# Three of four block sums of the spatial weights by adding DMA transfers in place of VectorE sums, in a fused attention and gated-MLP block on one Trainium2 core

## The chip, the core and the metric

The kernel runs on one NeuronCore of a Trainium2 chip. Such a core has five instruction streams that run at the same time and meet only through semaphores: TensorE (PE, matrix products into the accumulator memory PSUM; PEld is its weight load), VectorE (DVE, elementwise work), ScalarE (ACT, activation functions and copies), GpSimd (POOL, slower elementwise work, and issuer of transfers) and SyncE (SP, which here only issues DMA transfers). The working memory, SBUF, has 128 partitions. All five queues are in order: an instruction that waits holds up everything behind it on its engine.

The metric is the device time of one execution in microseconds, from an execution without the profiler, as the median of several; lower is better. Before the change: 227.09 us, median of 3 runs (226.91 to 227.54). The profiled execution has a time of its own, given below.

## The reference

One sequence of 2048 tokens with 512 features goes through two residual blocks, all in bfloat16:

```python
def _A_ref(x, wqkv, wo):                     # linear attention, 32 heads of 16
    q, k, v = split(x @ wqkv)
    phi = lambda t: jnp.where(t > 0, t + 1, jnp.exp(t)) + 1e-06
    pq, pk = (phi(q), phi(k))
    kv = jnp.einsum('bhsd,bhse->bhde', pk, v)
    z = jnp.einsum('bhsd->bhd', pk)
    o = einsum(pq, kv) / (einsum(pq, z) + 1e-06)
    return merge_heads(o) @ wo

def _B_ref(x, w_in, w_sp, b_sp, w_out):      # gated MLP, F = 1792, Fh = 896
    z = _gelu(jnp.einsum('bsd,df->bsf', x, w_in))
    z1 = z[..., :Fh].copy()
    z2 = _layernorm(z[..., Fh:], axis=-1)
    g = jnp.einsum('ts,bsf->btf', w_sp, z2) + b_sp[None, :, None]
    return jnp.einsum('bsf,fd->bsd', z1 * g, w_out)

h  = x + _A_ref(_layernorm(x), A_wqkv, A_wo)
h2 = h + _B_ref(_layernorm(h), B_w_in, B_w_sp, B_b_sp, B_w_out)
```

The change lies in the product of w_sp (2048 x 2048, the spatial weights, which mix tokens) with z2 (2048 x 896).

## The kernel before

Tokens are cut into 16 tiles of 128. In the first 65 us or so the attention block is done, tile by tile. Then come the input product with the two halves of w_in (z2 with its normalisation, and z1), the spatial mixing with the gate, and the output product with w_out. The last three stages overlap.

**Fewer products by sums.** The large products use a form of Strassen's scheme (Winograd's variant): a 2 x 2 block product is made of 7 block products instead of 8, at the price of sums of blocks. For w_sp, a row of tokens n (0 to 7) is taken together with row n + 8. Their transposed weights lie in SBUF as the tiles wt[n] and wt[n + 8], each 128 x 2048: the first half of the columns (index 0 to 7 of a 128-block) and the second (8 to 15). The program calls the four blocks y11 (wt[n], first half), y21 (wt[n], second), y12 (wt[n + 8], first) and y22 (wt[n + 8], second). It forms four sums of 128 x 1024 elements each with the helper `comb` (L859, whose DVE instruction the profile shows at L863):

- S1 = y12 + y22, into a tile of its own, sa[c][0];
- S2 = S1 - y11, into a second tile of its own, sa[c][1] (called q2);
- S3 = y11 - y12, in place into y12;
- S4 = y21 - S2, in place into y11.

The other operand has its own sums: zt1, zt2, zt4 and an in-place one in z2 (`t_sums`, L962).

**Pairs of rows.** `mix(ia, ib, nest)` (L1055) does two rows at a time, c = 0 and 1, in the order 0, 1 | 2, 3 | 7, 4 | 5, 6 (`MIX`); "tile n" below is the row pair n, n + 8. Each row has three PSUM banks, B, A and E. Bank A first gets y11 times z2, a copy of it goes to B (ACT), E gets S1 times zt1, B gets S2 times zt2 added ("the q2 product"), and so on; the last product of row n is y11 (by then S4) times the high half of z2, into E. The gate, z1 * (g + b_sp), reads the banks on DVE (L999, L1007, L1008), and each gated tile z1[n] is then transposed by a DMA transfer issued from SP (zgT[n], which lies over wt[n]) for the output product.

**A second level.** With a bit set in `NEST` (0, 3, 15, 7 for the four calls), one of the seven products is done for both rows together by `nested` (L1030), which applies the same scheme once more, with 224-column products and sums of its own: bit 1 reads y11 of both rows, bit 2 reads S1 of both, bit 4 reads y21, bit 8 reads y22. With bit 2 its last sum is written over the first half of sa[1][0], that is, over S1 of the second row.

**Order of the work.** Every operation is recorded by a helper with what it reads and writes, a cost and, for a transfer, a latency. The order in which the operations stand on each engine's queue is not computed in the kernel: it is unpacked from the string `ORDER` (L16), a list of operation numbers; the waits follow from the recorded reads and writes. A transfer has a semaphore by its name, and two transfers of one name share it: the two halves of wt[n] do, so a reader of either half waits for both. Since helpers record, one line stands for many operations in the profile (L427 all products, L446 all activations, L863 all of `comb`).

**Queues around the change.** SP issues all loads, the transposing loads of wt (L460), the zgT transfers and the stores. POOL does the small statistics steps of the normalisations (L541 to L575) and has nothing to do once the normalisation of z2 is over. DVE does the block sums, the additions of PSUM (L866, L1039), the statistics, and the gate.

Of the kernel before, what the change touches and what calls it, by code (L numbers as in the profile page):

```python
# [15 lines left out]
ORDER = "c-jrt)1oB^5Cgz;I%n?Kwr$(CZQHhO+qP}nwrzWMf1#c#93lV+4?{%6MGnM6E;xk92p~2hfk=cX$cd=Pjl@WRI7o;*$crRMfr3biXo!zsNQq=9gj6Vue29+ZNR9jmLOE1Gc~nFtq(ft*L1h#`2oynDWI%c}L=1#RMl?YqWI`1bMP@WbGgL(uR7W-xLp5YYH*`TvG)E1zL@l&JSJXrc6i0WIKyCCuYmCDfltd}CL3WfuY1Bba)J0qLLM)6&S+v7g^hP~Qz(gFzB=kW)ghYEx#z9QM5!A;a9K|toKwmV#Gz7;0^v6I<MMsRl2`s^I48k&WLKrN^QcTBb48{s{#t^K;NX*1)tiu_M!f~uZD1^lt%)n?Yz$~oCd@RITJjGB9!)(mKGc3YJEXD?G!gFlL4s6C2oWxw5!cNS?3+%-%?7=?l#(tc|OB}!}oWoX}#|3P|6<owhyNYYLj+?lJOSp_1SZi<b8n^Kt5AXr2>>cjlF7D$E?jg8^uyytk5p2C}uulkS5$z$?*jKE!ZwO<5@EO1H2$Ae3!dhs1j4ybCQ1%zF@A!de_6z?I-olv~EvCh?s20QAvRG`BMX{`w+5#5Yf>|2NX4x&sa#&tlZqY5R6|i`g&(c{=OJun$v8}N5R>tC5e9K@3t*phdBv#%ES$<1s8LhAtu?kkv5?DPeXGN`&)wWDl+3HwQYh}f(xYf7Z*4C0+Pit){tbtXry4KE0Su*QmsjRA{v^JL6df76oW(_Tm9kTY;!46vq`)Z|ag!Q$Nw$B<_NgHjAt+!3LBi7G4+9>O9W9+Cku^Cp=YS}EiYu{|P-M0PK)W%v1J7~vkoE@{7Hs0pg2^(N7ZGu&|JNCft*+V;N2kg6bvQswE?%N}KY^SY;4YX!9$S&F;cDBKG$>!QC`)%{=wf(gDcG<ev4{L5i?24VS1@^{BaFPwPvv!78?U%*kAA9>hduGO9Y<9H(Gtt@IV)C8E<zM?}L+y#3vtV3kSttfEINw_w#^VPYZapkMC)+jaW>YO3&s%sVU=Ai{2!6DumX#?Ofm7_6EwX8rjS;!TK3OehXD(i_NKDB*%*l|<$LF@#u3Kc@uux3J)XdEn)|Gi#gI$=PODzp+vLFlarWImc)@EqdVK=5_Le}F;>&3#{Xo(nwpRF{Dus(ZplXYhgmSJKx=VnXCvb<#txW#(1FT-#Eqp}6du@AQ~J-^siYsr2r%I%!PBuvUyoW*Sxjm6lX85ox3If&7@gB3WNtyz(SS&2Kjivu~A4OyJ?xtqy2gl#yK^SIp>a2Ut3EqB;LzGG!BVhJ{4V`k(^e&BE(V@aOi2#(`UTg>+y$yF@H@odK>tiq36%?Vt}PyEa;oXD?i!ZmEllbpo0oXk<&W$XBjqq&UVxtu>Zh3z?&NBEOt_?ri~o`3k4E4YEv*o+%_l)u=4@J*b~j@)fkd5ZsdjhktHoTqu1@`I%BG51S6&+EL*i#*4@7Vuym+=ILtx9}>@vJ+?U1|RbZZ!(1MVJN@A(0+>{{RzW)7!T|D{5HdTXYS=)M(~;3$EU2$%6^B>7|A1g6@S64jO<bTIqxx=NA(JRpV9pRWBN<R@P~}+H9eNc_Bj5EO_a-DGoDxX_+Hg(c|tGbkC?!-`5V^u>|VzUdr?p1xxIxF`&%aU9A3necrwrL#k{Vk@B+S{#XY&VQ7TXEZB@-vdI>M+^}LMd@%moF8>^(J@s=v<<vpiY^akEeP1V>-c|%X@rM;22_9ouOn|TZGqz;<o?Y*40@=Bi9J9$fQ?p-{cH}z(k;_bY-+H0CG@z(0<J$<@&RC=H69lWErQfKex%e|L()=Zz_-IT$5XpnmQTA%Hse5$YX0qUhye!$!MEbs4KG{^h+Qa|WjmC@Jv0w3dZJ(KrVUmvIeKF=5We9!FNy}Np9wD<6VKEyY8KOOR+K16H0uLk*g-{`A-sD^2iZ}vq#+=pwiU-l6itg*huw|hU|;iI(GS9lg5sa?L!uljBut(|_vkNOxL_Psts$9$Y_ct8_$+=uxHAL%DONGCk2k5vd=@jbrG$7`}qc`%*xeSY3&>a?HniJGR1e#t{>l5Y7Nz4o&{SGPTsW+}L)>ZZ@r1;69heXz&YHD91bdhGKRR<m{27wU~i(>Q<P?>)5k`zCEr9NqK98t+einO5k7zw^~vqE8-15B#lf)GAHzrCP3VTB(m7UTgKmKl?gGQe17(L%;7+G||6$Wc~E5`sOcuo4)%mf95}YyZ-nN{q^4-L8kahphuoi5tT@r6;C@AT`zr?b}NYz>!0t_0Y%lT|3i~hdz4bi6jQ~OO8u2whm}HUlu4;Y#ZqSNRW_wp7G>9d<<KGJR1{@ZZspPm<&o>4PU?(e=&X+Fm<lMbq%wN$=X6Q=R8U2fR{1qug;ZGQbwNc{R_Sz6C3RZGbXliVNmq1L*OWmwlu;#AO1Jeul~qnvbX}#jUN==<eN<JqR82MXNELKfb@fE|^i&m9UC&fgNAytj^jt4gOSSb%FZEgtR9}zvMsM{_4OK@U)JX63S)cS#KlD|9^jG)wO~(}>@KgVEM+jKpx4z2*zZ5aRfC66>IS>d03j_s11fm2Y1%d}c2BHR{1wsYZD0CofAY33!AbcQtAV%On@|lTd"  # L16
# [236 lines left out]
def bass_sequential_preLN__linear_attn_block__mixer_gmlp__prompt_kernel(  # L253
# [177 lines left out]
    def dve_cost(n, ps, acc=1):  # L431
        return n / acc / 0.96 + 58

    def act_cost(n, ps):
        return n / 1.2 + (49 if ps else 92)
# [23 lines left out]
    def dma_t(out_ap, in_ap, name, issue=1310.0, lat=1600.0, **k):  # L459
        return g.add("SP", lambda q: q.dma_start_transpose(out_ap, in_ap), [in_ap], [out_ap], cost=issue, lat=lat,  # L460
                     dma=name, **k)
# [56 lines left out]
    first_load("SP", wqkv[:, 0:2, D:2 * D], A_wqkv[0:2 * P, D:2 * D], "wka", 4200)  # L518
    wk = first_load("ACT", wqkv[:, 2:4, D:2 * D], A_wqkv[2 * P:4 * P, D:2 * D], "wkb", 4400)
    for n, lat, behind in ((4, 4600, None), (6, 3400, x2), (8, 3850, wk), (10, 4000, wk), (12, 4200, wk), (14, 4400, wk)):  # L520
        load_x("SP", n, 2, lat, behind)
# [11 lines left out]
    def stats(src, k, n):  # L533
        s = st[k][:, n, :]
        dve(lambda v: v.bn_stats(s[:, 0:6], src[:, n, :]), [src[:, n, :]], [s[:, 0:6]], D)  # L535
        return dve(lambda v: v.bn_aggr(s[:, 6:8], s[:, 0:6]), [s[:, 0:6]], [s[:, 6:8]], 14)
# [19 lines left out]
    def moments(s, col, n):  # L556
# [3 lines left out]
             [s[:, 2:3]], 240)  # L560
        pool(lambda p: p.tensor_scalar(ve, s[:, 2:3], s[:, 1:2], EPS_LN, op0=ALU.add, op1=ALU.add), [s[:, 1:3]], [ve], 240)
        pool(lambda p: p.tensor_scalar(mean, s[:, 0:1], 1.0 / n, None, op0=ALU.mult), [s[:, 0:1]], [mean], 190)
# [11 lines left out]
    def rpow(ve, r):  # L574
        pool(lambda p: p.tensor_tensor(r, ve, expo[:, 0:1], ALU.pow), [ve, expo], [r], 620)  # L575
# [25 lines left out]
    def phi(dst, b, w=2, split=False):  # L601
# [4 lines left out]
        dve(lambda v: v.tensor_scalar(e, e, 1.0, EPS_PHI, op0=ALU.min, op1=ALU.add), [e], [e], w * GW, acc=4)  # L606
# [624 lines left out]
```

## Time and profile before

| what | value |
|---|---|
| time, median of 3 runs | 227.09 us (226.91 to 227.54) |
| profiled execution: its time | 227.38 us |
| profiled execution: span from first to last instruction | 225.5 us |
| PE busy | 218.1 us (97%) |
| DVE busy | 204.9 us (91%) |
| ACT busy | 138.0 us (61%) |
| POOL busy | 51.5 us (23%), last instruction near 115 us |
| granted TensorE clock | 1.000 |
| one sum of 128 x 1024 on DVE (L863) | 0.69 us |
| one load of half a wt tile (256 KB), issue to landing | 4.1 us median, 3.4 to 7.9 |

How to read it: "busy" is the time in which an engine's instructions ran, and an instruction that waits counts as idle. A group line gives the source line, the engine, the operation, what it writes and reads (tile names without their numbers) with partitions x elements, how many there were, and then busy us and mean ns of one, and after the next bar the engine's idle time just before them. In a timeline the time in brackets is the idle time before and what ended it. L numbers are lines of the kernel before. The products' ends are modelled, so a product's duration is longer than the distance to the next one; the distance between starts is what TensorE needs.

### The profile page before, as it was taken

The numbers are of one execution on the slowest core, as the hardware profiler recorded it, in microseconds if no ns is written. First come the engines' busy times: TensorE is split into PE (matmuls) and PEld (weight loads), VectorE is DVE, ScalarE is ACT, GpSimd is POOL, SyncE is SP. The second block draws the span as 40 slices with busy tenths as digits, with TensorE's granted clock in tenths as the row PEclk, the third lists the DMA queues.
The fourth block names the chain that finished last, engine by engine and source line by source line (L and its number), as shares of the span: only waits on it lengthen the run. The fifth ranks groups of instructions, "written<-read, shape, count | busy, mean of one in ns | idle before, by whom it ended". The sixth has DMA issues, their size and how long they took to land.

```text
span 225.5 us, 3882 instructions
## 1 busy us (share of the span) xinstructions
PE 218.1 (97%) x1361; PEld 125.6 (56%) x1361; DVE 204.9 (91%) x473; ACT 138.0 (61%) x274; POOL 51.5 (23%) x134
## 2 busy tenths in 40 slices
PE   8899999999999999999999999999999999999995
PEld 7434444453334454544555555767678668885653
DVE  4899855699999999989999999999999999999884
ACT  5686735479969999999675335543235824664111
POOL 2455400000384874597720000000000000000000
PEclk9999999999999999999999999999999999999999
DMA  5736478936553344699990225999061520262474
GB/s 160 241 104 150 75 209 246 241 70 159 125 116 70 70 93 74 132 174 184 217 199 7 41 44 103 182 181 132 0 128 34 97 58 9 65 67 87 85 188 148
DMA packets 73907, 26.87 MB, mean 119 GB/s; under 512 B 63648, under 2 KB 73888, under 8 KB 73888
## 3 DMA queue, kind: packets, MB, share of 16 engines
q1 hardware_dynamic: 73184, 26.03, 54.8%
q10 hardware_dynamic: 704, 0.59, 0.9%
q8 instruction: 11, 0.18, 0.3%
q14 instruction: 8, 0.07, 0.1%
HBM read 6.95 MB, written 2.10 MB: 40 GB/s over the span
## 4 chain that ended last, share of the span: by engine, by line
PE 66%; ACT 13%; DVE 8%; POOL 5%; DMA 4%; issue 2%; SPq 1%; ACTq 0%
PE psum L427 59%; PE psum L684 6%; ACT z L446 3%; DMA x<-in_A_x_dram 3%; DVE h L829 2%; ACT z1t L446 2%; ACT sq L446 2%; POOL rs L575 2%; DMA zgT<-z1t 1%; DVE st L535 1%; ACT psum L446 1%; ACT p5z L446 1%; DVE h L1170 1%; ACT sh L446 1%; ACT ct L446 1%
## 5 line engine op out<-in xcount | busy, mean ns | idle before, releaser
L446 ACT ACTIVATE psum<-psum 128x448 f32<-128x448 f32 (+2 forms) x76 | 31.5, 425 | 36.6 <-PE psum L427 29.7
L427 PE MATMUL psum<-z,wt 128*128 128x448 bf16 (+1 forms) x216 | 41.9, 335 | 0.0
L427 PEld LDWEIGHTS psum<-z,wt 128*128 128x128 bf16 x216 | 21.1, 98 | 14.9
L427 PE MATMUL psum<-win,hnT 128*128 128x448 bf16 x112 | 26.3, 353 | 0.0
L446 ACT ACTIVATE e<-psum 128x1024 bf16<-128x1024 f32 (+1 forms) x18 | 16.7, 928 | 14.1 <-PE psum L427 13.6
L446 ACT ACTIVATE z1t<-psum 128x448 bf16<-128x448 f32 (+1 forms) x24 | 16.2, 678 | 12.7 <-PE psum L427 9.9
L427 PE MATMUL psum<-zt,sa 128*128 128x448 bf16 (+1 forms) x120 | 22.2, 321 | 0.0
L427 PE MATMUL psum<-ws,hs 128*128 128x448 bf16 x72 | 19.0, 353 | 0.0
L446 ACT ACTIVATE p<-psum,b 128x448 f32<-128x448 f32 x22 | 13.5, 633 | 6.2 <-PE psum L427 4.3
L427 PEld LDWEIGHTS psum<-win,hnT 128*128 128x128 bf16 x112 | 10.5, 98 | 10.9 <-ACT z1t L446 0.9
L427 PE MATMUL psum<-xnT,wqkv 128*128 128x512 bf16 x64 | 15.6, 379 | 0.2 <-DVE pqT L611 0.2
L866 DVE TENSOR_TENSOR psum<-psum,p5z 128x448 f32<-128x448 f32 x24 | 15.1, 628 | 0.9 <-PE psum L427 0.4
L427 PE MATMUL psum<-wqkv,xnT 128*128 128x512 bf16 x64 | 15.4, 379 | 0.4 <-DMA wqkv<-in_A_wqkv_dram 0.4
L427 PE MATMUL psum<-m,pqT 128*128 128x512 bf16 x64 | 15.0, 380 | 0.7 <-DVE h L829 0.7
L427 PE MATMUL psum<-wout,zgT 128*128 128x256 bf16 (+1 forms) x77 | 15.2, 302 | 0.2 <-DVE h L1170 0.2
L427 PEld LDWEIGHTS psum<-zt,sa 128*128 128x128 bf16 x120 | 11.7, 98 | 6.5
L684 PE MATMUL psum<-pk,xn 128*128 128x512 bf16 x64 | 15.3, 379 | 0.0
L446 ACT ACTIVATE z<-psum 128x896 bf16<-128x896 f32 x16 | 14.9, 946 | 0.5 <-PE psum L427 0.2
L427 PE MATMUL psum<-nv,nu 128*128 128x224 bf16 x108 | 14.4, 259 | 0.0
L1007 DVE TENSOR_TENSOR u<-psum,p 128x448 bf16<-128x448 f32 x22 | 13.7, 622 | 0.5 <-PE psum L427 0.3
L606 DVE TENSOR_SCALAR e<-e 128x1024 bf16<-128x1024 bf16 (+1 forms) x18 | 7.1, 397 | 7.4 <-ACT e L446 7.2
L559 POOL TENSOR_SCALAR st<-st 128x1 f32<-128x1 f32 x10 | 4.2, 422 | 40.9 <-ACT sh L446 36.5
(147 smaller groups left out, 455.1 us busy)
## 6 DMA issues: line engine op xcount, KB each, us to landing
r<-rcp SPq DMA_DIRECT2D x16, 128.0 KB, 2.6
out_dram<-h SPq DMA_DIRECT2D x15, 128.0 KB, 1.9
win<-in_B_w_in_dram SPq DMA_DIRECT2D x2, 896.0 KB, 6.1
x<-in_A_x_dram SPq DMA_DIRECT2D x6, 256.0 KB, 4.2
wqkv<-in_A_wqkv_dram SPq DMA_DIRECT2D x2, 512.0 KB, 4.2
wout<-in_B_w_out_dram SPq DMA_DIRECT2D x1, 896.0 KB, 6.2
wo<-in_A_wo_dram SPq DMA_DIRECT2D x1, 512.0 KB, 4.9
wt<-in_B_w_sp_dram SPq DMA_TRANSPOSE x32, 4.1
```

The costliest lines, as they stand in the source:

```text
L427: inst = pe.matmul(out_ap, lhsT=a, rhs=b, start=start and i == 0, stop=stop and i == len(pairs) - 1, **kw)
L446: return g.add("ACT", lambda ac: ac.activation(out_ap, in_ap, func, **kw), [in_ap, *extra], [out_ap] + ([accum] if accum is not None else []),
L535: dve(lambda v: v.bn_stats(s[:, 0:6], src[:, n, :]), [src[:, n, :]], [s[:, 0:6]], D)
L559: pool(lambda p: p.tensor_scalar(s[:, 2:3], s[:, 0:1], s[:, 0:1], -1.0 / (n * n), op0=ALU.mult, op1=ALU.mult), [s[:, 0:1]], [s[:, 2:3]], 240)
L575: pool(lambda p: p.tensor_tensor(r, ve, expo[:, 0:1], ALU.pow), [ve, expo], [r], 620)
L606: dve(lambda v: v.tensor_scalar(e, e, 1.0, EPS_PHI, op0=ALU.min, op1=ALU.add), [e], [e], w * GW, acc=4)
L684: inst = pe.matmul(bank(CB[c]), lhsT=xn[:, i, c * P:(c + 1) * P], rhs=pk[:, i, :], start=i == 0, stop=i == NT - 1)
L829: dve(lambda v, n=n, b=b, s=s: v.scalar_tensor_tensor(h[:, n, :], bank(b), 1.0, x[:, n, :], op0=ALU.mult, op1=ALU.add, accum_out=s[:, 0:1] ...
L866: dve(lambda v: v.tensor_tensor(half(b), half(src), p, ALU.add), [half(src), p], [half(b)], HW, ps=True)
L1007: dve(lambda v: v.tensor_tensor(u, half(b), p, ALU.add), [half(b), p], [u], HW, ps=True)
L1170: dve(lambda v, o=o, q=q, add=add: v.tensor_tensor(o, q, add, ALU.add), [q, add], [o], DH2, ps=True)
```

## The change

Of the four sums of each of the eight tiles, S1 stays on DVE. The three others are made by DMA transfers that add to their destination, issued from POOL (`add_dma`), and all of them in place:

- transfer 1: y12 += y11 (waits for S1, which reads y12);
- transfer 2: y11 += S1 (waits for transfer 1 and for every other reader of y11); the result takes the place of q2, so sa[c][1] is no longer used;
- transfer 3: y11 += y21, after the q2 product has read y11.

These transfers add, so signs are turned: the sums become the negatives of the old ones where needed, the copies of banks A to B and B to E are made with scale -1 (`copy_neg`), one of the two bias activations too, and one operand order in `t_sums` is turned. The number and the shapes of the matrix products stay. `DACC` sets for each of the four calls which of the three sums go by transfer; it is 7 (all) in each.

Besides: each half of a wt tile has a semaphore of its own; the recorded costs and latencies are changed (they enter only the order in which several waits of one operation stand); a second way for the gate on ACT is added but not used (`GACT` is empty); and `ORDER` is a new list, for the whole kernel. In the new list the first 700 of 1306 places differ from the old ones by small exchanges; from there on the q2 product and the last products of a row stand elsewhere, with other products between them.

```diff
@@ load_w
-            op = dma_t(wt[n][:, j:j + HT, :], ..., f"wt{n}", issue=1350, lat=2900)
+            op = dma_t(wt[n][:, j:j + HT, :], ..., f"wt{n}_{j}", issue=1350, lat=2900)
...
+    copy_neg = lambda o, i: act(o, i, ACT.Copy, HW, scale=-1.0)
...
@@ t_sums
-        comb(z2[:, a, hi], z2[:, b, hi], z2[:, a, hi], ALU.subtract)
+        comb(z2[:, a, hi], z2[:, a, hi], z2[:, b, hi], ALU.subtract)
...
+    DACC = (7,7,7,7)
...
+    def add_dma(dst, src_ap):
+        nm = f"acc{acc[0]}"
+        acc[0] += 1
+        g.add("POOL", lambda q: q.dma_start(dst, src_ap, accum_op=ALU.add), [dst, src_ap], [dst], cost=1100.0, lat=3300.0, dma=nm)
+
-    def mix(ia, ib, nest):
+    def mix(ia, ib, nest, by_dma):
...
-            copy(half(B), half(A))
+            copy_neg(half(B), half(A))
             comb(sa[c][0], y12, y22, ALU.add)
-            comb(sa[c][1], sa[c][0], y11, ALU.subtract)
+            if by_dma & 1:
+                add_dma(y12, y11)
+            else:
+                comb(y12, y12, y11, ALU.add)
+            if by_dma & 2:
+                add_dma(y11, sa[c][0])
+            else:
+                comb(y11, y11, sa[c][0], ALU.add)
...
-            q1, q2 = sa[c]
+            q2 = y11
             pa, pb = p5[c]
-            for t, p in ((tl, pa), (th, pb)):
-                act(p, half(E), ACT.Identity, HW, bias=b32[:, t:t + 1], extra=[b32[:, t:t + 1]])
-            comb(y12, y11, y12, ALU.subtract)
-            comb(y11, y21, q2, ALU.subtract)
+            for t, p, sign in ((tl, pa, -1.0), (th, pb, 1.0)):
+                act(p, half(E), ACT.Identity, HW, bias=b32[:, t:t + 1], scale=sign, extra=[b32[:, t:t + 1]])
             matmuls(half(B), [(q2[:, s, :], zt2[:, s, :]) for s in ss], **onto)
+            if by_dma & 4:
+                add_dma(y11, y21)
+            else:
+                comb(y11, y11, y21, ALU.add)
...
-            copy(half(E), half(B))
+            copy_neg(half(E), half(B))
...
-        mix(MIX[k], MIX[k + 1], NEST[k // 2])
+        mix(MIX[k], MIX[k + 1], NEST[k // 2], DACC[k // 2])
```

More of the change, by code (lines that the diff above doesn't have):

```diff
@@ L517, in bass_sequential_preLN__linear_attn_block__mixer_gmlp__prompt_kernel @@
     load_x("ACT", 3, 1, 2550)
-    first_load("SP", wqkv[:, 0:2, D:2 * D], A_wqkv[0:2 * P, D:2 * D], "wka", 4200)
-    wk = first_load("ACT", wqkv[:, 2:4, D:2 * D], A_wqkv[2 * P:4 * P, D:2 * D], "wkb", 4400)
-    for n, lat, behind in ((4, 4600, None), (6, 3400, x2), (8, 3850, wk), (10, 4000, wk), (12, 4200, wk), (14, 4400, wk)):
+    first_load("SP", wqkv[:, 0:2, D:2 * D], A_wqkv[0:2 * P, D:2 * D], "wka", 5050)
+    wk = first_load("ACT", wqkv[:, 2:4, D:2 * D], A_wqkv[2 * P:4 * P, D:2 * D], "wkb", 5280)
+    for n, lat, behind in ((4, 5330, None), (6, 4150, x2), (8, 3100, wk), (10, 3280, wk), (12, 4150, wk), (14, 4350, wk)):
         load_x("SP", n, 2, lat, behind)
@@ L995, in bass_sequential_preLN__linear_attn_block__mixer_gmlp__prompt_kernel @@
                 z1_tile(n, 6)
+    cnt = [0]
     def gate(n, c, b):
         o = z1[n][:, c]
-        dve(lambda v: v.scalar_tensor_tensor(o, half(b), b32[:, n:n + 1], o, op0=ALU.add, op1=ALU.mult),
-            [half(b), b32[:, n:n + 1], o], [o], HW, ps=True)
-    cnt = [0]
+        if n in GACT:
+            u = u_t[cnt[0] % 2]
+            cnt[0] += 1
+            act(u, half(b), ACT.Identity, HW, bias=b32[:, n:n + 1], extra=[b32[:, n:n + 1]])
+            dve(lambda v: v.tensor_tensor(o, u, o, ALU.mult), [u, o], [o], HW, acc=2)
+        else:
+            dve(lambda v: v.scalar_tensor_tensor(o, half(b), b32[:, n:n + 1], o, op0=ALU.add, op1=ALU.mult),
+                [half(b), b32[:, n:n + 1], o], [o], HW + 60, ps=True)
     def gate_p(n, c, b, p):
```

34 lines of the change are left out of this document (18 added, 16 removed).

## The prediction

> **What bounds the kernel now.** I read the page first: busy time by engine, then the windows by stage, the list of waits, the chain that ended last, and last the groups by shape and the DMA rows.
>
> The page's first part (busy us, share of the span, instructions) and the line of the mean DMA load:
>
> ```profile
> PE 218.1 (97%) x1361; PEld 125.6 (56%) x1361; DVE 204.9 (91%) x473; ACT 138.0 (61%) x274; POOL 51.5 (23%) x134
> DMA packets 73907, 26.87 MB, mean 119 GB/s; under 512 B 63648, under 2 KB 73888, under 8 KB 73888
> ```
>
> TensorE has 7 us free in the whole span. The windows (stretch, length, then PE, PEld, DVE, ACT, POOL busy, granted clock, DMA share, GB/s) say where:
>
> ```profile
> 66.00:100.00 34.00, 34.00 (x175) 16.16 (x174) 32.91 (x85) 33.23 (x68) 22.80 (x54) 1.00 0.50 100
> 100.00:105.00 5.00, 4.50 (x24) 2.01 (x23) 4.56 (x12) 4.85 (x9) 3.36 (x9) 1.00 0.99 180
> 105.00:135.00 30.00, 30.00 (x162) 15.61 (x161) 29.69 (x60) 17.09 (x33) 7.61 (x16) 1.00 0.58 108
> 135.00:145.00 10.00, 9.45 (x73) 6.68 (x72) 9.65 (x23) 5.98 (x16) 0.00 (x0) 1.00 0.80 128
> 145.00:216.00 71.00, 71.00 (x526) 50.79 (x525) 69.03 (x174) 30.79 (x75) 0.00 (x0) 1.00 0.45 84
> ```
>
> DVE is 97 to 99% busy from 105 us on, and yet PE never stops from 105 to 135 and from 145 to 216. So DVE is full, but it is not late. PE is dense too, not only counted as busy: in the timeline groups of eight 448-column products start 1.51 us apart, 0.19 us each, one behind the other.
>
> ```profile
> 118.07 1.68 PE L427 MATMUL psum<-z,wt 128*128 128x448 bf16 x8
> 119.58 1.68 PE L427 MATMUL psum<-zt,sa 128*128 128x448 bf16 x8
> ```
>
> The same view gives 0.10 us for a 224-column product and 0.11 for 256. The two gaps after 66 us, from the chain that ended last (start, us, what):
>
> ```profile
> 102.67 0.33 issue
> 103.00 0.64 DVE psum L866
> 103.64 0.05 issue
> 103.68 30.08 PE psum L427 x158
> ...
> 134.50 3.27 DMA zgT<-z1t
> ...
> 137.84 0.56 ACT z1t L446
> ...
> 138.42 0.64 DVE psum L866
> ```
>
> The first comes out of the normalisation of z2 (from 94.4 to 101.0 us the chain runs almost wholly on POOL, the last steps on DVE). The second is not DVE's: a transposing transfer of a gated tile frees the slot into which ACT writes the next z1 tile, and DVE and PE wait behind that. After 66 us, then, the windows show 0.50 + 0.55 = 1.05 us without a product running. That, and not DVE's 98%, is what a lighter DVE could win.
>
> **The change, part by part.** *Sums taken off DVE.* Of each tile's four sums one stays (y12+y22). The three others are these groups (with the kept one, 4 x 8):
>
> ```profile
> L863 DVE TENSOR_TENSOR wt<-wt,sa 128x1024 bf16<-128x1024 bf16 x8 | 5.5, 690 | 0.0
> L863 DVE TENSOR_TENSOR wt<-wt,wt 128x1024 bf16<-128x1024 bf16 x8 | 5.5, 686 | 0.0
> L863 DVE TENSOR_TENSOR sa<-sa,wt 128x1024 bf16<-128x1024 bf16 x8 | 5.4, 689 | 0.0
> ```
>
> 24 x 0.69 = 16.5 us leave DVE (204.9 to about 188.4). On the path: the products in between keep their number and shapes, so PE's 218 us stay. Bounds: 0 (no gap is released by these sums) to -1.05 (both gaps close). I take -0.4, nearer to 0, since one gap hangs on POOL and the other on a transfer.
>
> *Signs.* Copies with scale -1 and one operand order turned: the same instructions as the 543 and 633 ns rows of ACT; 0. *Own semaphores for the halves of a weight row:* waits can only end earlier; no wait on these loads shows on PE; 0.
>
> *24 adding transfers, their issue.* POOL has no instruction after 115 us, so 21 of the 24 issues meet an idle queue. The first three (transfer 1 of tiles 0 and 1, transfer 2 of tile 0) stand by the new order among the normalisation's steps, where POOL is the chain. An issue there holds back the steps behind it. Bounds per issue: 0 (fits a gap) to 1.3 us (the longest usual issue row, SP's transposes; SP's plain ones take 0.6). One of the three I count, the one that falls in the stretch from 94 to 101 us, at the plain 0.6: **+0.6**, range 0 to 3.9. Behind it wait rstd, the z2 normalisation on DVE, the add of L866 and the product that was already late at 103 us.
>
> *How long a transfer takes.* No row shows an adding transfer or one from POOL. Nearest rows (us from issue to landing):
>
> ```profile
> r<-rcp SPq DMA_DIRECT2D x16, 128.0 KB, 2.6
> x<-in_A_x_dram SPq DMA_DIRECT2D x6, 256.0 KB, 4.2
> wt<-in_B_w_sp_dram SPq DMA_TRANSPOSE x32, 4.1
> ```
>
> A sum writes 256 KB and must read 512 KB. From below: 2.6, the SBUF-to-SBUF row. From above: 7.9, the slowest weight load (that tile's view gives 3.4/4.1/7.9). Between: 2.6 plus three further 128 KB at the best slice's 246 GB/s, 1.6 us, is 4.2; 0.3 more, one small POOL instruction, for the other queue: 4.5 us quiet. Beside weight loads, where the DMA share is 0.8 to 1, I add 0.8 (the loads' median over their fastest is 0.7): 5.3.
>
> [...]
>
> *What waits for them.* Each tile's chain is now: sum on DVE, transfer 1, transfer 2, product with q2, transfer 3, last product of its row. In place means that transfer 2 also waits for every reader of y11, and transfer 3 for the q2 product. PE runs in order, so a late landing stops it whole. The cover is what the new order places between release and use, in products times the 0.19, 0.10 and 0.11 us above:
> - tile 0, transfer 3: 26 products of 448 columns, 4.9 us; weight and w_out loads run beside it: 5.3 - 4.9 = 0.4 late.
> - tile 2, transfer 2: from the last nested sum that reads y11, 12 of 224, one of 512 (0.2), 3 of 256 and 16 of 448: 4.7; eight weight loads run: 0.6 late.
> - tile 2, transfer 3: 24 of 224, 9 of 256, 8 of 448: 4.8; 0.5 late.
> - tile 3, transfer 3: 4.85, and the 0.5 just lost lies inside it: 0.
> - tile 7, transfer 3: 5.6; tiles 1 and 4 more: 0 in quiet queues.
> - tile 6, transfers 1 and 2 in series between its DVE sum and its q2 product: 9.3 against 2 x 4.5: 0. In the same place DVE itself waits: a nested sum overwrites the tile that transfer 2 reads; its queue holds evictions behind it.
>
> Sum: **+1.5**. Bounds: 0, if a landing takes 4.5 everywhere, to +9.7 with 6.5 everywhere (1.6 + 1.8 + 1.7 + 0.9 + 3.7).
>
> *New order elsewhere.* The first 700 places differ by small exchanges. Gaps of PE from 45 to 70 us are about 1 us in sum; an order can close or open as much: 0, range -0.7 to +0.7.
>
> Together -0.4 + 0.6 + 1.5 = +1.7. The profiled execution took 227.38 (span 225.5 and 1.9 around it), 0.3 above the median of 227.09; the median is what the forecast goes with: 228.8.
>
> **The rivals.** *In time (faster).* Landings at or below 4.5 even beside the loads: no product is late. Then -0.4, and with -0.7 from a better order: 226.0. For it: all three rows above are below 4.5, and DVE has 16 us more to evict sooner. Against: PE has no gap to give in 135 of the last 150 us. It decides at a landing of 4.7 us. The same landings with POOL's price give no change, 227.1 to 227.5. [...]
>
> *Late everywhere (much slower).* POOL's instructions stretch beside DVE's long SBUF operations. Two rows of one line in the POOL timeline:
>
> ```profile
> 103.23 0.31 POOL L561 TENSOR_SCALAR st<-st 128x1 f32<-128x1 f32 x1
> 104.80 1.63 POOL L561 TENSOR_SCALAR st<-st 128x1 f32<-128x1 f32 x1
> ```
>
> The second ran beside a 1.04 us DVE sum. If an issue stretches by 1.3 us as that row did, quiet landings are 5.8 and loaded ones 6.6: 1.7 + 1.9 + 1.8 + 0.2 + 2.3, and 1.3 in the normalisation, minus 0.4: +8.8, 235.9; with half the stretch 231.8. For it: DVE is never free. Against: the stretched rows read SBUF, an issue may not. [...]
>
> *It does not do what it says*: the page after would show DVE still near 205 us. The code leaves no way to that, under 1 in 100.
>
> **How the numbers follow.** About 0.3% (0.7 us) is what a measurement here can tell from no change: faster is below 226.4, slower above 227.8. Landing near 5 us with one or two late products (228 to 231): 0.43. Late everywhere, above 231: 0.16. In time and faster: 0.27. In time but given back on POOL or by order, within 0.7: 0.14. So faster 0.27, same 0.14, slower 0.59. Time 228.8; the range 225.8 to 232.8 leaves out the best of the first rival and the worse half of the second, together under 2 in 10. The forecast's own range is 227.8 to 231.
>
> **What the profile after would show.** DVE near 188 us and POOL with 24 issues: the first term. PE gaps with a DMA of wt as releaser, at the q2 product of tile 2 and the last rows of tiles 0 and 2: the third; their landing row near 4.5 to 5.3. A larger gap near 103 us behind POOL: the second. It would be wrong if landings are below 4.5 (PE's gaps then as few as before, time at or below 227), or above 6, when the wait for transfers leads the list of PE's waits and DVE's queue shows one too, at the nested sum.

## The result, and the profile after

The kernel after takes 235.04 us (median of 4 executions, 233.38 to 237.13) where the kernel before, beside it, took 227.22: a ratio of 1.0321 (95% interval 1.0274 to 1.0367). The forecast was 228.8 with a range up to 232.8. The profiled execution of the kernel after is the longest of the four, 237.13 us with a span of 235.4; that of before had 225.5. Ratios here and below leave out executions more than 1.5% above the fastest of the same kernel, the profiled one of after among them, so they can lie below the quotient of two medians. Where I give a loss in us without more, it is the ratio less 1, times 227.0 (here 7.3 us).

The page's first part (busy us, share, instructions), the granted clock in 40 slices, and the packets of the new queue:

```profile
PE 221.2 (94%) x1347; PEld 127.2 (54%) x1361; DVE 193.3 (82%) x449; ACT 137.8 (59%) x274; POOL 70.7 (30%) x158
...
PEclk9999999999999999999998999989999999999999
...
q0 software_dynamic: 3456, 6.29, 17.7%
```

DVE lost 24 instructions and 11.6 us of busy time, POOL has 24 more, so the change did what it says. (The sums after are not simply the negatives of those before: S1 - y11 has become S1 + y11, and y11 - y12 has become y12 + y11. The weights of row n now count as negated, and the copies, one bias and one operand order make up for it.) The durations of all DVE instructions added up fall by 18.2 us (240.5 to 222.3), where 24 x 0.69 is 16.5; busy time falls by less because neighbouring instructions overlap in the records. New in the clock digits are two that are not 9.

The windows (stretch, length, PE, PEld, DVE, ACT, POOL busy, granted clock, DMA share, GB/s):

```profile
95.00:115.00 20.00, 20.00 (x108) 10.15 (x106) 19.68 (x44) 17.14 (x33) 17.58 (x31) 1.00 1.12 186
115.00:130.00 15.00, 12.06 (x56) 5.68 (x55) 10.10 (x20) 5.50 (x12) 3.49 (x4) 0.89 0.93 181
130.00:150.00 20.00, 18.33 (x121) 11.14 (x121) 14.90 (x32) 9.65 (x23) 1.10 (x2) 1.00 0.58 108
150.00:165.00 15.00, 11.94 (x71) 7.44 (x69) 8.77 (x22) 4.63 (x11) 3.39 (x5) 0.89 1.00 139
165.00:226.00 61.00, 60.27 (x449) 43.59 (x452) 51.98 (x136) 25.55 (x63) 9.32 (x11) 1.00 0.70 131
```

PE, which before had no gap from 105 to 135 and from 145 to 216 us, is idle for 2.9 us in the second row and for 3.1 in the fourth, and in both the mean clock is 0.89. From 165 us on, where 10 of the 24 transfers are issued, it is nearly as dense as before (0.7 us idle of 61). The lists of PE's and of DVE's waits (us in total, times, longest) name the cause:

```profile
PE psum L427 <- DMA wt<-sa: 6.0, 2, 3.1
PE psum L427 <- DVE psum L866: 2.0, 3, 1.5
...
DVE sa L863 <- DMA wt<-sa: 5.5, 2, 4.0
```

The transfer wt<-sa is transfer 2. The q2 product of tile 1 waits 3.1 us for it (118.4 to 121.5 us), that of tile 2 3.2 us (152.3 to 155.5), counted from when the next product could have started; the modelled ends lie about 0.15 us later, so the records show 2.9 and 3.1. DVE waits where the nested sum overwrites S1. Finer windows, first and third the pauses, second and fourth the time behind them:

```profile
118.00:121.40 3.40, 0.52 (x3) 0.08 (x1) 1.87 (x4) 1.59 (x3) 0.86 (x1) 1.00 1.16 171
...
122.50:125.90 3.40, 3.40 (x11) 1.38 (x10) 0.76 (x3) 0.98 (x2) 1.90 (x3) 0.51 0.29 50
...
152.00:155.50 3.50, 0.48 (x3) 0.04 (x1) 2.06 (x5) 0.00 (x0) 0.00 (x0) 1.00 1.29 116
156.60:160.00 3.40, 3.40 (x17) 2.27 (x15) 1.43 (x4) 1.16 (x2) 0.86 (x1) 0.50 1.06 211
```

Behind each pause the granted clock is at half for 3.4 us: 448-column products then start 0.37 us apart instead of 0.19, so each stretch costs 1.7 us more. The gap near 142 us (the chain from the transfer of z1t8) is 1.6 us instead of 0.5. Together that is 3.1 + 3.2 + 2 x 1.7 + 1.1 = 10.8 us, against 9.9 by the spans; the 0.9 between the two was not placed. The other three executions had a mean clock of 0.992 to 0.993, one half-clock stretch each by this measure (0.5 x 3.4 / 233 = 0.007), the profiled one 0.985, two.

Both stretches have the same length in the trace, 3.413 us (122.45 to 125.86 and 156.58 to 159.99 us); the pauses ahead of them are 3.1 and 3.2 us. What brings the half clock on is asked in the last group of runs.

The DMA rows of the two stretches, 113.6 to 121.5 us and 147.3 to 158.1 (packets, MB, share of 16 engines; then KB each and median us to landing):

```profile
q1 hardware_dynamic: 2824, 1.40, 69.5%
q0 software_dynamic: 261, 0.47, 43.8%
...
wt<-sa POOLq DMA_DIRECT2D x1, 256.0 KB, 7.8
...
wt<-in_B_w_sp_dram SPq DMA_TRANSPOSE x2, 8.8
```

```profile
wt<-sa POOLq DMA_DIRECT2D x2, 256.0 KB, 8.2
...
wt<-in_B_w_sp_dram SPq DMA_TRANSPOSE x6, 6.5
```

Both transfers run beside loads, and the loads beside them are slow too (8.8 us, where the median of before was 4.1). With no packet of the loads' queue beside it, or 7 at most, a transfer lands in 3.3 to 3.6 us (those issued at 124.0, 162.9, 181.6, 183.1 and 213.2 us). At tile 1 most of the delay lies ahead of the first packet. From 115.7 to 118.4 us the loads' queue is the only one that ran a packet:

```profile
q1 hardware_dynamic: 1384, 0.81, 115.2%
```

The transfer's own packets begin at 118.5 us, 4.9 us after its issue at 113.6. Those of the transfer issued at 124.0 us, with nothing beside it, begin after 1.4 us.

### The profile page after: what moved, and what is told of

Read it like the earlier page. It is cut to its first block, busy times and chain, and to the rows that moved or that the text cites. A ratio compares the mean times of both kernels' runs of the same rounds, so it can differ in the third digit from the quotient of the medians.

```text
span 235.4 us, 3883 instructions
## 1 busy us (share of the span) xinstructions
PE 221.2 (94%) x1347; PEld 127.2 (54%) x1361; DVE 193.3 (82%) x449; ACT 137.8 (59%) x274; POOL 70.7 (30%) x158
## 4 chain that ended last, share of the span: by engine, by line
PE 65%; DMA 11%; issue 10%; DVE 8%; ACT 3%; POOL 1%; SPq 1%; POOLq 0%
PE psum L427 58%; PE psum L684 6%; DMA wt<-sa 3%; DMA x<-in_A_x_dram 2%; DMA wt<-wt 2%; DMA zgT<-z1t 2%; DMA hnT<-hn 2%; DVE h L1194 1%; DVE st L535 1%; DVE st L944 1%; ACT ct L446 1%; ACT e L446 1%; POOL wt L1068 1%; DVE psum L866 1%; DVE nu L863 1%
## 5 line engine op out<-in xcount | busy, mean ns | idle before, releaser
L446 ACT ACTIVATE psum<-psum 128x224 f32<-128x224 f32 (+2 forms) x76 | 30.6, 422 | 35.1 <-PE psum L427 30.6
L427 PE MATMUL psum<-z,wt 128*128 128x448 bf16 (+1 forms) x216 | 42.4, 340 | 0.1
L427 PE MATMUL psum<-zt,wt 128*128 128x448 bf16 (+1 forms) x120 | 25.6, 357 | 6.0 <-DMA wt<-sa 6.0
L1068 POOL DMA_DIRECT2D wt<-wt x16 | 14.2, 989 | 45.9 <-PE psum L427 45.1
L427 PE MATMUL psum<-win,hnT 128*128 128x448 bf16 x112 | 25.6, 353 | 0.0
L427 PEld LDWEIGHTS psum<-zt,wt 128*128 128x128 bf16 x120 | 11.7, 99 | 15.7 <-DMA wt<-sa 6.9
L1068 POOL DMA_DIRECT2D wt<-sa x8 | 7.0, 871 | 37.2 <-DVE nu L863 20.7
L866 DVE TENSOR_TENSOR psum<-psum,p5z 128x448 f32<-128x448 f32 x24 | 14.9, 624 | 3.8 <-PE psum L427 2.6
L427 PE MATMUL psum<-xnT,wqkv 128*128 128x512 bf16 x61 | 15.0, 379 | 0.4 <-issue 0.2
L559 POOL TENSOR_SCALAR st<-st 128x1 f32<-128x1 f32 x10 | 3.2, 317 | 39.1 <-ACT sh L446 35.3
```

The lines of the kernel that those rows point to most:

```text
L427: inst = pe.matmul(out_ap, lhsT=a, rhs=b, start=start and i == 0, stop=stop and i == len(pairs) - 1, **kw)
L446: return g.add("ACT", lambda ac: ac.activation(out_ap, in_ap, func, **kw), [in_ap, *extra], [out_ap] + ([accum] if accum is not None else []),
L559: pool(lambda p: p.tensor_scalar(s[:, 2:3], s[:, 0:1], s[:, 0:1], -1.0 / (n * n), op0=ALU.mult, op1=ALU.mult), [s[:, 0:1]], [s[:, 2:3]], 360)
L866: dve(lambda v: v.tensor_tensor(half(b), half(src), p, ALU.add), [half(src), p], [half(b)], HW, ps=True)
L1068: g.add("POOL", lambda q: q.dma_start(dst, src_ap, accum_op=ALU.add), [dst, src_ap], [dst], cost=1100.0, lat=3300.0, dma=nm)
```

## The experiments

The theory at this point: two transfers that land late beside loads, and the half clock behind them, are the loss; the lighter DVE is worth nothing. Against it stood the new order, a cost of every transfer, and POOL held up by DVE.

### Sums back on DVE, in all or half of the calls

```diff
-    DACC = (7,7,7,7)
+    DACC = (0,0,0,0)      # first; second: (0,0,7,7), third: (7,7,0,0)
```

> The kernel after, its order, signs and in-place sums, but with all 24 sums back on DVE as additions (DACC 0 in all four calls). Theory: the loss of 7.8 us comes from two transfers that land late at the q2 products of tiles 1 and 2, and from a TensorE clock at half for 3.4 us behind each of these two pauses. Then both pauses over 3 us go, the granted clock stays 1.00, and the time is 227 to 229.5 us (some loss may stay, since each sum now stands on DVE's queue where its transfer stood on POOL's, and the gap at 142 us is not a transfer's of POOL). Rival, the new order itself costs it: 232 us or more, with PE's pauses at the same places.

> The kernel after with adding transfers only in the last two calls (rows 7, 4 and 5, 6), sums on DVE in the first two. Theory: those 12 transfers land in 3.3 to 4.9 us within their cover, no pause comes from them: within 1 us of the kernel with all sums on DVE, 226.5 to 229.5 us. Rival, each transfer costs something wherever it stands (POOL's issue or the transfers slow DVE or PE): about half the loss, 230 to 232 us.

> The kernel after with adding transfers only in the first two calls (rows 0, 1 and 2, 3), sums on DVE in the last two. Theory: both late landings stand in these calls, so the whole loss stays: 233 to 236 us, two pauses of about 3 us and a granted clock of 0.50 for 3.4 us behind each. Rival, a cost per transfer: 230 to 232 us.

Measured: 233.89 us, 1.0296 (1.0281 to 1.0312); 230.41, 1.0134 (1.0110 to 1.0159); 235.54, 1.0353 (1.0314 to 1.0391). The first was a miss: without any adding transfer the kernel is still 6.7 us slower. The second was one too: it lies where the rival put it. The third met its time by luck: in its profile no pause was longer than 2 us and the clock was 1.00 throughout, so the loss did not come from two long pauses and a halved clock. The windows of the first show DVE nearly as full as before and PE no longer dense:

```profile
105.00:145.00 40.00, 36.55 (x205) 18.81 (x205) 36.01 (x73) 20.01 (x42) 6.32 (x12) 1.00 0.53 103
145.00:216.00 71.00, 68.17 (x504) 47.57 (x503) 66.67 (x168) 31.05 (x77) 0.00 (x0) 1.00 0.40 79
```

So these three could not tell the new order from a sum that stands badly in it: a sum that waited on POOL's empty queue now stands on DVE's, ahead of evictions. Hence the next group, which takes the sums away altogether.

### Sums left out

```diff
     def add_dma(dst, src_ap):
...
+        if len(g.ops) in LEFT_OUT:     # in short: all | transfer 2 of tiles 1 and 2 | first two calls | first | second
+            w = warm[:, 4 * acc[0]:4 * acc[0] + 4]
+            g.add("POOL", lambda q: q.memset(w, 0.0), [], [], cost=1100.0)
+            return
```

> The kernel after with the 24 transfers replaced by as many small memsets on POOL: 24 of the 32 sums of spatial-weight blocks are not made, by no engine, so the products read blocks that were not summed; products and order are as in the kernel after. It bounds what taking the sums off DVE could bring at best. Theory: DVE was full but not late, so 226.0 to 228.0 us, at most 1 us below the kernel before. Rival, DVE's 16.5 us were worth something that the late landings hide: 224.5 us or less. Rival, the new order costs it: 231 us or more.

> The kernel after with two of its 24 transfers left out (transfer 2 of tile 1 and transfer 2 of tile 2, each replaced by a small memset; the q2 products of these two rows read a block without its sum). Order, loads and the other 22 transfers are as in the kernel after. Theory, these two late landings and the halved clock behind them are the loss: 227 to 229.5 us, no pause above 2 us, clock 1.00. Rival, the loss is spread over all transfers, or the next one in each chain becomes late instead: 231.5 us or more.

> The kernel after with the 12 transfers of the first two calls left out (small memsets in their place), the 12 of the last two calls as they were. It shows what the late 12 cost without sums on DVE in the way. Theory, nothing: 226.5 to 228 us. Rival, a cost per transfer: 230 us or more.

> The kernel after with the 6 transfers of the first call (rows 0 and 1) left out, the other 18 as they were. The early twelve cost 6.9 us (235.0 against 228.1 with them left out). Theory, each call has one chain that comes late beside loads, so each carries about half: 230.5 to 232.5 us, one pause of 2 to 3.5 us at the q2 product of tile 2 left and at most one half clock. Rival, one call carries it all: below 229.5, or above 234.

> The kernel after with the 6 transfers of the second call (rows 2 and 3) left out, the other 18 as they were. Theory: 230.5 to 232.5 us, the pause of 2 to 3.5 us at a q2 product of the first call left. Rival: below 229.5, or above 234. If the shares add, the two times stand above 228.1 by 6.9 us together.

| left out | time, us | ratio (95%) | loss, us |
|---|---|---|---|
| none (the kernel after) | 235.04 | 1.0321 (1.0274 to 1.0367) | 7.3 |
| all 24 | 226.86 | 0.9991 (0.9968 to 1.0013) | -0.2 |
| first two calls | 228.11 | 1.0061 (1.0036 to 1.0085) | 1.4 |
| first call | 228.13 | 1.0051 (1.0021 to 1.0082) | 1.2 |
| second call | 230.95 | 1.0148 (1.0097 to 1.0199) | 3.4 |
| two single transfers | 232.72 (227.6 to 234.9) | - | - |

The row with all 24 left out answers two questions at once. In the new order and without the 24 sums the time is that of the kernel before: taking the sums from DVE for nothing at all, in this order, wins nothing, and with the sums gone the order costs nothing. That the order costs a little and the lighter DVE wins as much is not excluded; the order of before with the sums left out was not run. The windows of that run show PE as dense as before from 145 us on (71.00 of 71 us) with DVE at 86%; the gap that the kernel after has near 142 us is there too, 1.9 us at 138:

```profile
115.00:145.00 30.00, 27.91 (x171) 15.96 (x170) 24.45 (x48) 14.47 (x32) 0.00 (x0) 1.00 0.40 79
145.00:216.00 71.00, 71.00 (x528) 50.88 (x526) 60.85 (x159) 30.80 (x77) 0.00 (x0) 1.00 0.42 85
```

So in this order no way of making these sums elsewhere would have gained more than 0.7 us, the far end of that interval.

The early twelve cost 7.3 - 1.4 = 5.9 us, the late twelve 1.4 to 1.6. By the spans the late twelve cost 0.7 (median 225.8 against 225.1); the rest lies ahead of the first or behind the last instruction. The shares of the two early calls do not add: with the first call's transfers gone (228.1, a miss), those of the second cost nothing more than the late twelve; with the second's gone (as expected), the first's cost 2.0. That speaks for the second call's being late only when the first call was, but why is open: transfer 2 of tile 2 meets the same eight loads in both cases and was issued 5 us after the first of them in both, and landed in 4.9 us in the one profile and in 8.2 in the other. And it is not always late behind a late first call: in the profile with transfers in the first two calls only, transfer 2 of tile 0 took 7.8 us and that of tile 2 4.8. Leaving out two single transfers was a miss as a test. Its four executions scatter from 227.6 to 234.9; in the profiled one, of 231.5, transfer 2 of tile 0, in time before, took 8.1 us and the q2 product of tile 0 waited:

```profile
PE psum L427 <- DVE psum L866: 2.4, 3, 1.8
PE psum L427 <- DMA wt<-sa: 2.3, 1, 2.3
```

So it is not two certain transfers that are late but, from one execution to the next, others in the chain of the first two calls. Kernels whose early transfers meet loads scatter by 2.5 to 7.3 us over four to six executions (two executions at a mean clock below 0.95, of 243 and 287 us, not counted). That with all sums on DVE scatters by 0.4 over four, that with the sums left out by 2.0 over ten. (Of the one with only the late transfers and sums on DVE, three lie within 1 us and one is 5 us longer.)

### The loads moved, or made otherwise

```diff
+    g.ops[446].deps.add(714)    # w_out (and wt7 behind it) after transfer 2 of tile 1
+    g.ops[815].deps.add(855)    # wt5, wt13 after transfer 2 of tile 3
```

> The kernel after with two waits added on SP: the load of w_out (and the two loads of wt7 behind it) starts only when transfer 2 of tile 1 has landed, and the loads of wt5 and wt13 only when transfer 2 of tile 3 has. Theory, the loads that run beside them make the transfers late: transfer 2 of tile 1 lands in 4 to 5.5 us instead of 7.8, the pause of 3.1 us at its q2 product shrinks to at most 1; that of tile 2 lands in 5 to 6.5 instead of 8.2 (the loads of wt4 and wt12 still run beside it), its pause to 0.5 to 1.5; the granted clock stays 1.00; 228.5 to 231 us. A new wait on a load may give back up to 1. [...]

The same with one tile in other memory:

```diff
-    z1 = [... o_xnT + slot[n] * ZR ...]
+    z1 = [... o_xnT + slot[n] * ZR if n != 14 else o_win + KD * FH * 2 ...]
```

> As the kernel with the later loads, and the tile z1t14 moved from the memory of z1t8 into that of q2 of row 0, which the change left unused. Theory: the gap near 142 us (ACT waits with z1t14 until the transfer of z1t8 has read it, and the sum of L866 and PE behind it; 0.54 us in the kernel before, 1.6 in the kernel after) goes, so 1 to 2 us less than with the later loads alone: 227 to 229.5 us. Rival, another wait ends the same gap (the sum of L866 waits for its product anyway): within 0.5 us of the later loads alone.

Plain loads in place of transposing ones:

```diff
-            op = dma_t(wt[n][:, j:j + HT, :], B_w_sp[...], ...)
+            op = dma("SP", wt[n][:, j:j + HT, :], B_w_sp[...].rearrange("p (a b) -> p a b", a=HT), ...)   # n in W3 + W4
```

> The kernel after with the 16 loads of wt7, wt15, wt4, wt12, wt5, wt13, wt6 and wt14 as plain transfers of 256 KB with rows of 2 KB instead of transposing ones: the same bytes, but these weights are not transposed, so the spatial product of half of the rows is another one. Theory, it is the small packets of the transposing loads that fill the DMA engines: transfer 2 of tile 2 lands in 4 to 5.5 us, its pause goes, transfer 2 of tile 1 (beside w_out and wt7) in 5 to 7; 229 to 232 us. Rival, bytes in flight alone matter: landings near 8 us at tile 2, 233 us or more. Rival, POOL beside DVE: the same 233 or more.

Later loads: 235.40 us, 1.0329 (1.0252 to 1.0405); with z1t14 moved 234.76, 1.0308 (1.0244 to 1.0372): no gain, a miss in the time. (The profile of the first, of 286.6 us at a mean clock of 0.757, is not used. That of the second is of its longest execution, 243.0 us at 0.937, and what it shows need not hold for the other three, of 232.6 to 235.2.) In the profile of the second, transfer 2 of tile 1 landed in 3.4 us instead of 7.8 and its pause was gone; but the load of w_out now met transfer 3 of tile 0, which took 8.2 us, and PE stopped for 3.7 us at the last product of tile 0 instead. In that execution the collision had only been moved. With z1t14 in its own memory ACT no longer waited for the transfer of z1t8, and yet the gap stayed at 1.1 us: DVE's queue has the sum us<-zgT ahead of L866, and that waits for a transfer of zgT too. The rival held for the tile that was moved.

Plain loads: 232.70, 1.0212 (1.0144 to 1.0280), between the theory's upper end and the rivals. Transfer 2 of tile 1 took 6.7 us, that of tile 2 7.8 and not 4 to 5.5, its first packet 4.6 us after the issue. So it takes no small packets of transposing loads to make a transfer late; loads of 2 KB rows do it as well.

Then the load of w_out alone, and all the loads of the first call's time, without touching the order of PE or DVE (in all three, the load of w_out is also no longer tied to the weight loads before and behind it):

```diff
+MOVES = ((446, 347),)                               # first run: w_out issued near 72 us
+MOVES = ((446, 203), (701, 726), (702, 701))        # second and third run: w_out near 31 us, wt7 behind transfer 3 of tile 1
+    g.ops[701].deps.add(726)
+    g.ops[815].deps.add(855)                        # third run only
```

> The kernel after with only the load of w_out (0.92 MB) moved from 111 us to about 72 us, where the DMA share was 0.16. Theory, transfer 2 of tile 1 then runs beside the two loads of wt7 alone: it lands in 5 to 6.5 us instead of 7.8, its pause of 3.1 us shrinks to 0.5 to 2; tile 2 as before: 232 to 234 us. Rival, w_out is not what delays it: 235 us; or w_out delays the transposing transfers of hn at 72 us and with them the products: above 236.

> The kernel after with the load of w_out issued near 31 us, ahead of the value weights, and the loads of wt7 only after transfer 3 of tile 1 has landed; nothing else moved. Beside the transfers of rows 0 and 1 then run only the last loads of wt3 and wt11. Theory: transfer 2 of tile 1 lands in 3.5 to 5 us, its pause of 3.1 us falls to 0.5 or less, transfer 3 of tile 0 lands in 3.3 to 4 us; the pause at tile 2 and one half clock stay: 230 to 232 us. Rival, another wait takes the place of the pause: 233 us or more.

> The same, and the loads of wt5 and wt13 only after transfer 2 of tile 3 has landed. Theory: transfer 2 of tile 2 lands in 4.5 to 5.5 us instead of 8.2, its pause falls to 0 to 1; transfer 3 of tile 2, which now meets these loads, may be late by 1 to 2: 228.5 to 231 us, and clock 1.00. Rival, the collision is only moved: as the run before it or above.

Measured: w_out at 72 us 231.51, 1.0178 (1.0132 to 1.0225); the first call quiet 231.90, 1.0144 (1.0124 to 1.0164); both 232.58, 1.0224 (1.0166 to 1.0282). The second is the cleanest test. Its windows from 113 to 121 us, and its DMA rows from 113 to 117:

```profile
113.00:117.00 4.00, 4.00 (x23) 2.07 (x22) 3.90 (x9) 2.82 (x6) 1.35 (x2) 1.00 0.89 163
117.00:121.00 4.00, 4.00 (x23) 2.06 (x21) 3.96 (x8) 2.29 (x5) 1.67 (x3) 1.00 0.38 66
```

```profile
q0 software_dynamic: 288, 0.52, 73.5%
q1 hardware_dynamic: 535, 0.13, 15.5%
...
wt<-sa POOLq DMA_DIRECT2D x1, 256.0 KB, 3.3
```

The same transfer, issued at the same time (113.5 us), beside a DVE that is 98% busy, lands in 3.3 us instead of 7.8, and PE has no gap. Of what runs in that stretch only the load traffic was changed. This refutes POOL being held up by DVE, and shows the loads as the cause of this late landing. The issue itself took 0.89 us in both kernels. The kernel regains 4.0 of the 7.3 us (by the median spans of all four executions 4.3: 229.0 against 233.3). It does not regain all: SP now holds the transfer of z1t0 behind the waiting loads, and the wait that was hidden under the pause shows (timeline: start, us, and the idle time before):

```profile
127.00 1.30 SPq L464 DMA_TRANSPOSE zgT<-z1t  x1
...
130.59 0.54 ACT L450 ACTIVATE z1t<-psum 128x448 bf16<-128x448 f32 x1 [4.58 <-DMA zgT<-z1t]
131.17 0.63 DVE L868 TENSOR_TENSOR psum<-psum,p5z 128x448 f32<-128x448 f32 x1 [2.24 <-ACT z1t L450]
...
131.86 0.55 PE L431 MATMUL psum<-ws,hs 128*128 128x448 bf16 x2 [1.75 <-DVE psum L868]
```

and transfer 3 of tile 2 now lands in 6.5 us, 2.1 late, with a half clock behind it in the profiled execution. In the third run, a miss, the loads that were to make the second call quiet met transfer 3 of tile 3: 8.6 us, a pause of 4.3: the rival, a collision that is only moved. With w_out at 72 us (faster than expected in time), transfer 2 of tile 1 took 6.1 us beside the weight loads and that of tile 0 7.9, and the transposing transfers of hn were late in turn (a gap of 1.9 us at 80 us).

### More products as cover

```diff
+MOVES = ((725, 779), (726, 725), (741, 745), (742, 741), (743, 742), (875, 870), (886, 929), (887, 886))
```

The second run has these moves, w_out near 72 us, and the waits of wt7, wt5 and wt13 of the runs above.

> The kernel after with only the order changed around the two late places: the q2 products of tiles 1 and 2 stand 2.7 and 2.2 us of other products later, and so that transfer 3 behind them does not become late in turn, the last products of these rows (with their gate steps) 2.3 and 2.2 us later. Every load and transfer is as it was. Theory, a late landing costs what exceeds its cover: the pauses of 3.1 and 3.2 us shrink to about 0.5 and 1, the granted clock stays 1.00, 228.5 to 231 us. Rival, the lateness moves down the chain (transfer 3 starts only when the later q2 product is done): the pauses come back at the last products, 232 us or more. Rival, the loss is not of the cover: 234 us or more.

> Both together, and the loads of wt7 only after transfer 3 of tile 1 has landed, those of wt5 and wt13 after transfer 2 of tile 3. All sums still go by transfers. Theory: no pause above 1 us behind a transfer is left; what stays of the loss is the gap near 142 us: 226.8 to 229 us, at best the time with the sums left out (226.9), so no gain over the kernel before. Rival, something of the transfers beyond late landings costs time (their packets beside loads and transposes, POOL's issue): 230 us or more.

Measured: 238.04 us, 1.0412 (1.0307 to 1.0518), and 243.35, 1.0734 (1.0672 to 1.0796), both misses on the far side. The waits of the second:

```profile
PE psum L431 <- DVE psum L868: 7.4, 4, 5.0
PE psum L431 <- DMA wt<-wt: 2.2, 1, 2.2
...
DVE u L1017 <- PE psum L431: 13.6, 10, 6.5
```

All six transfers of its first call landed in 3.2 to 5.1 us and none was waited for by PE; the wait for transfers is down to one of 2.2 us. But the gate steps of the moved product stand on DVE's queue where they wait for PE, the evictions behind them wait, and PE waits for those: 5.2 us in one piece. In the first run's profile PE's two long pauses, 2.7 and 2.6 us with a half clock behind each, are waits for DVE too, which in the second of them had itself waited 2.3 us for a transfer. The idea of more cover was not tested by this, only that order.

### How long a pause halves the clock

```diff
+    for a, b, k in ((779, 741, 3), (919, 886, 4), (1034, 987, 5), (1086, 1101, 6)):
+        ops = [pool(lambda p: p.memset(pad, 0.0), [], [pad], 400) for _ in range(k)]
+        ops[0].deps.add(a)
+        g.ops[b].deps.add(ops[-1].i)
```

> The kernel before with four pauses of TensorE and nothing else: a chain of 3, 4, 5 and 6 memsets on POOL (each writes the same unused 736 bytes of a partition) stands between two products that were dense, near 125, 150, 175 and 200 us; estimates of the pauses from the memset rows of before: 2.0, 2.5, 3.1 and 3.7 us. Theory, a pause of about 3 us lowers the granted clock to 0.50 for 3.4 us and so costs 1.7 us more than its length, one of 2 us costs its length only: 227.3 + 11.3 + 3.4 = 242 us, with the granted clock at 0.50 behind the third and the fourth. Rival, the clock fell for another reason (DMA load, or both engines on SBUF): clock 1.00 throughout, 238.6 us.

Measured: 238.44 us. The pauses were 1.6, 2.1, 2.5 and 3.0 us, shorter than estimated; 227.3 + 9.2 + 1.7 = 238.2, with one half-clock stretch, behind the third, and none behind the longer fourth. So a pause alone does it, without adding transfers, and neither the theory ("about 3 us") nor the rival held.

What decides is where the pause falls. In every profile of this case the granted clock changes only at whole multiples of 3.413 us from its first change (in this run after 52, 53 and 68 of them; in the kernel before after 65; in the kernel after after 34, 35, 44, 45 and 67), so these traces show a fixed grid of windows, and its place can be read from each. On that grid the second, the third and the fourth pause, the last cut by a boundary, look like this (the third row is the window behind the third pause, the sixth the time behind the fourth):

```profile
151.75:155.17 3.42, 1.51 (x13) 0.96 (x11) 3.42 (x10) 0.63 (x1) 1.62 (x4) 1.00 0.82 184
179.06:182.47 3.41, 1.04 (x8) 0.47 (x6) 3.41 (x11) 1.94 (x4) 2.02 (x5) 1.00 0.77 144
182.47:185.88 3.41, 3.41 (x16) 2.05 (x15) 0.37 (x2) 0.37 (x1) 0.00 (x0) 0.50 0.00 0
206.36:209.78 3.42, 2.27 (x22) 1.83 (x19) 3.14 (x11) 2.26 (x6) 0.97 (x3) 1.00 0.40 76
209.78:213.19 3.41, 1.73 (x10) 0.99 (x11) 3.38 (x10) 0.82 (x2) 1.45 (x4) 1.00 0.68 178
211.60:215.00 3.40, 3.40 (x24) 2.17 (x23) 2.14 (x5) 0.91 (x2) 0.00 (x0) 1.00 0.15 49
```

PE is idle for 1.9 us in the window of the second pause (full clock behind it), for 2.4 in that of the third (half clock behind it), and for 1.2 and 1.7 in the two windows that share the fourth (full clock). Over the profiles of this case at a full clock otherwise, between 6 and 215 us: of 33 windows at full clock with 1.0 to 1.91 us of idle PE none was followed by half clock, of 10 with 1.98 us or more all were. In the kernel after the two windows ahead of the half clock, 119.03 to 122.45 and 153.17 to 156.58 us, hold 2.4 us of idle PE each. In length, pauses of 2.1 to 3.0 us went either way, six of ten; by idle time within a window the 43 part without an exception.

## Why the prediction was wrong

- **What bounds the kernel; DVE's relief, -0.4 (0 to -1.05): right, as far as tested.** In the new order, with all sums gone, the gain is 0.2 us (0.7 to a loss of 0.3), within the bound of PE's 1.05 us of gaps. DVE's busy time fell to 193.3 us and not to 188, since overlapping durations do not subtract one for one.
- **Issues in the normalisation, +0.6: nothing seen.** The issues took 0.9 to 1.07 us. But the gap they were to lengthen, 0.5 us at 103 us before, stands at 92.5 us in the new order (0.4 us, with the sums left out too), ahead of the first issue at 95.5.
- **Landings, +1.5: the mechanism right, the sizes wrong, and this is the step that failed.** That transfers beside loads stop PE in order at the q2 product of tile 2 is what happened, with 3.2 us where 0.6 was forecast. In the kernel after a quiet landing is 3.3 to 3.6 us, not 4.5, and a loaded one 4.1 to 8.3, not 5.3. By the run with the sums left out, all that the transfers do costs 7.3 + 0.2 = 7.5 us. The 0.8 added for loads was the spread of the loads among themselves; the row that showed what loads do to one another, 7.9 for the slowest, was taken as a bound and not as what two queues beside each other give. The upper end of that term, +9.7, holds what was measured; the range of the forecast, up to 232.8, left it out.
- **"Tiles 1 and 4 more: 0 in quiet queues": wrong for tile 1.** Its transfer 2 was issued at 113.6 us, behind POOL's normalisation steps (transfer 1 had landed at 111.1), just as w_out and wt7 were loading (DMA share 1.12 and more), took 7.8 us and cost 3.1. The windows of before had shown a DMA share of 0.99 in 100 to 105 us; from 105 on only the mean of 30 us was read, 0.58. In windows of 5 us it is 0.94 to 1.09 from 105 to 120, and the mean hid that.
- **Transfer 3 of tile 0, 0.4 late:** it landed in 5.3 us, as forecast, but under the pause at tile 1, and cost nothing.
- **Transfer 3 of tile 2, 0.5 late** (its products add up to 4.9 us of cover, not 4.8): it landed in 4.6 us and no pause shows; it came out as 2.1 us late when the first call was made quiet.
- **A term that was missing: the clock.** Every pause was priced at its length. In the kernel after, one or two of them per execution cost 1.7 us more.
- **Order, 0 (-0.7 to 0.7): nothing against it** (-0.2 together with DVE's relief, with the sums left out), though the gap of the zgT transfer grew by 1.1 us in the kernel after.
- **The rivals.** "In time" named its point well, a landing of 4.7 us, and is what happened from 165 us on (landings of 3.3 to 4.9 us there). "Late everywhere" gave 235.9, near the 235.0 measured, but for another reason: no issue was stretched from 165 us on (0.86 us each, and 0.89 behind the one before it where two came at once), those before 115 us by some 0.2 at most, and a landing beside a DVE that is 98% busy took 3.3.
- **What would show it wrong** was met: landings above 6, the wait for transfers at the head of PE's list, and a wait of DVE at the nested sum.

## What to carry to other kernels

Before work is taken off a full engine, run the kernel with that work left out: here that shows in one run that 16.5 us of DVE's time, in the new order, are worth 0.2. A transfer that takes the place of an instruction in a dependent chain must be priced by its landing beside the loads of its own stretch, read from short windows and not from a mean over 30 us; and here moving a load, a wait or a product out of one collision made the next (a transfer of 8.2 us, one of 8.6, evictions that PE waited 5.2 us for), since what stands behind a waiting instruction on its queue waits too. In this case a pause that leaves TensorE idle for some 2 us or more within one 3.4 us window of its clock costs 1.7 us on top of its length.

## What the runs showed of the hardware that was not expected

- An adding transfer of 256 KB (bf16, memory to memory on the chip) lands in 3.3 to 3.6 us in the kernel after with at most 7 packets of the loads' queue beside it, and in 3.7 where that queue has a share of 0.1 to 0.2, with DVE 36 to 100% busy meanwhile. Of three issued one behind the other (at 124.0 us) the landings were 3.4, 4.3 and 5.2 us, some 1.4 us after one another. Beside more loads: 4.1 to 8.3 in the kernel after, up to 8.6 in the other runs, and 9.4 for one queued behind two others. Its 16 completion signals come within 0.2 us when quiet (124.0 us), and over 3.3 us, from 152.2 to 155.5, beside the loads.
- Beside each other both were slow: transfer 2 of tile 1 took 7.8 us and the two loads 8.8, where a quiet transfer took 3.3 to 3.6 and the median load of before 4.1. No packet of the transfer ran from 115.7 to 118.4 us, while 1384 of the loads' did; the trace does not tell whether its packets were ready by then, so how the two queues share the DMA engines is not shown. Why one execution gives 4.9 and another 8.2 for the same transfer stays open, as do the 1.4 us of the late twelve.
- In these traces TensorE's clock goes by a fixed grid of 3.413 us windows: 1.98 us of idle time or more within one halved the clock of the next (10 of 10), 1.91 or less did not (0 of 33). A pause of 3.0 us that a boundary of the grid cut in two left the clock full.
